# A grouped 1x1 convolution on one core: the small piece that only some DMA engines carry becomes larger and is shared with GpSimd's queue

## The chip, the core and the metric

The kernel runs on one core of a Trainium2 chip. The metric is the device time of one execution in microseconds (us), lower is better; the kernel before takes 485.12 us, the median of three runs that lie between 485.1 and 485.2. A core has TensorE for matmuls (PE in the profile), VectorE (DVE), ScalarE (ACT), GpSimd (POOL) and SyncE (SP), and its transfers between main memory and the on-chip memory are carried out by 16 DMA engines. An engine that issues a transfer puts it on a queue of its own; the 16 DMA engines work the queues off.

## The reference, cut to what matters

```python
H = W = 512; G = 4; Cg = 48; C = 192; k = 1
xg = x.reshape(B, H, W, G, Cg)                 # B = 1, bf16
out[..., g, :] = einsum('bhwc,cd->bhwd', xg[..., g, :], w[0, 0, :, g, :])
```

Each of 262,144 pixels has 192 channels in four groups of 48, and each group is multiplied by its own 48 x 48 matrix. A pixel is 384 bytes, so 100.66 MB are read and as many are written; the weights are small.

## The kernel before, in words

**Pieces.** All pixels are cut into pieces (`plan_pieces`, L67 to L86). A piece of n columns is a block of 128 rows (SBUF partitions) by n pixels; a column is thus one pixel in each of 128 rows. The middle of the image goes in pieces of 104 columns (`BIG`), ahead of them stand small head pieces of 8, 20 and 32 columns that share the first slot, so that work can begin early. One piece is different: the narrow one (`NARROW`, L32 to L34) has 48 columns but only 32 rows, 0 to 15 and 32 to 47, and each of its two 16-row blocks is handed over with a leading dimension of four (`a=4`, L114), so that four DMA engines carry it, 8 rows each. It stands in slot 10. With it the full pieces have 60 + 19 x 104 = 2036 columns instead of 2048; the 16 DMA engines carry those 2036 columns in equal shares, 8 rows each, and four of them another 48 columns' worth.

**The ring.** SBUF holds a ring of five slots of 104 columns (`ring`, L129). A slot is loaded, computed in place (the result is written over the input) and stored from.

**Queues.** SP issues all loads in order (L170 to L175); ahead of the load of slot n it waits until all stores of slot n - 5 have landed (L173). ACT issues all stores (`store`, L250 to L254) between its copies. Most pieces are stored with one transfer, the five slots before the last with two halves of 52, and the last slot in parts of 32, 32, 24 and 16 (L117 to L124). GpSimd only prepares two constants at the start (L155 to L162) and issues no transfer.

**Compute.** A group is 4 columns. For each group PE transposes six 128 x 128 blocks (L203), DVE copies the transposed blocks of a pair of groups to SBUF (L242), PE multiplies them by the weights (L218), and ACT copies the result over the input in the ring (L260). There are 521 groups. The first group of a piece waits for the load of the piece (L198). The narrow piece's 12 groups are computed with all 128 rows, though only 32 hold data.

Of the kernel before, what the change touches and what calls it, by code (L numbers as in the profile page):

```python
# [6 lines left out]
BF16 = mybir.dt.bfloat16  # L7
# [4 lines left out]
C = GROUPS * CG  # L12
# [11 lines left out]

BIG = 104
RCOLS = 5 * BIG
HEAD = (8, 20, 32)
LATE = 6
LATE_PARTS = (52, 52)
LAST_PARTS = (32, 32, 24, 16)  # L30
FULL = ((0, 128),)
NARROW = ((0, 16), (32, 16))  # L32
NARROW_COLS = 48
NARROW_AT = (9,)  # L34
NXP = 4
NXS = 3
NOB = 4
# [2 lines left out]
class Waiter:  # L40

    def __init__(self, eng):
        self.eng = eng
        self.seen = {}
# [5 lines left out]
        self.eng.wait_ge(sem, val)  # L50


class Piece:

    def __init__(self, i, slot, at, g0, size, blocks, pix):
        self.i, self.slot, self.at, self.size = i, slot, at, size
        self.g0, self.g1 = g0, g0 + size // 4
        self.full = blocks is FULL
        self.blocks = []
        for (r0, rows) in blocks:  # L60
            self.blocks.append((r0, rows, pix))
            pix += rows * size
        self.pix_end = pix
        assert size % 4 == 0 and self.at + size <= RCOLS


def plan_pieces(npix):  # L67
    few = NARROW_COLS * sum(rows for _, rows in NARROW)
    at = [i for i in NARROW_AT if npix >= len(NARROW_AT) * few + 128 * (sum(HEAD) + BIG * (i + 2))]
    cols = (npix - few * len(at)) // 128  # L70
    assert cols % 4 == 0
    head = list(HEAD) if cols >= sum(HEAD) + BIG else []
    mid = cols - sum(head)
    slots = [[(BIG, FULL)]] * (mid // BIG) + ([[(mid % BIG, FULL)]] if mid % BIG else [])
    for i in at:
        slots.insert(i, [(NARROW_COLS, NARROW)])
    if head:
        slots.insert(0, [(s, FULL) for s in head])
    pieces, g, pix = [], 0, 0
    for n, parts in enumerate(slots):  # L80
        c = n * BIG % RCOLS
        for s, blocks in parts:
            pieces.append(Piece(len(pieces), n, c, g, s, blocks, pix))
            c, g, pix = c + s, pieces[-1].g1, pieces[-1].pix_end
    assert pix == npix
    return pieces  # L86


def bass_standalone__grouped__vision_kernel(nc, x, w, out):
    B, H, W_, Cx = x.shape  # L90
    assert Cx == C and tuple(w.shape) == (1, 1, GROUPS, CG, CG)
    npix = B * H * W_
    assert npix % 512 == 0, "the pixel count must be a multiple of 512"

    pieces = plan_pieces(npix)
# [4 lines left out]
    xf = x.rearrange("b h w c -> (b h w) c")  # L100
    of = out.rearrange("b h w c -> (b h w) c")
# [2 lines left out]
    def groups(pair):  # L104
        return range(2 * pair, min(2 * pair + 2, NG))

    def transfers(ap, ring, p, c0=0, c1=None):
        c1 = c1 or p.size
        for (r0, rows, pix) in p.blocks:
            px = ap[pix:pix + rows * p.size, :]  # L110
            if p.full:
                view = px.rearrange("(p i) n -> p (i n)", p=rows)[:, c0 * C:c1 * C]
            else:
                view = px.rearrange("(c a i) n -> a c (i n)", a=4, c=rows // 4)  # L114
            yield view, ring[r0:r0 + rows, (p.at + c0) * C:(p.at + c1) * C]

    stores = []  # L117
    for p in pieces:
        late = pieces[-1].slot - p.slot
        parts = LAST_PARTS if late == 0 else LATE_PARTS if late < LATE else (BIG,)  # L120
        c = 0
        for n in parts if p.size == BIG and p.full else (p.size,):
            stores.append((p, c, c + n, p.g0 + (c + n) // 4))
            c += n  # L124
    st_val = {p: 16 * sum(len(p.blocks) for q, *_ in stores if q is p) for p in pieces}

    with ExitStack() as es:
        block = es.enter_context(nc.Block())
# [9 lines left out]
        def sem(name):  # L138
            return es.enter_context(nc.semaphore(name))

        ld_sem = [sem(f"ld{p.i}") for p in pieces]
        st_sem = [sem(f"st{p.i}") for p in pieces]
        w_sem, id_sem, e_sem, wb_sem, wc_sem = (sem(s) for s in ("w_sem", "id_sem", "e_sem", "wb_sem", "wc_sem"))
        p0_sem, p1_sem = sem("p0_sem"), sem("p1_sem")
        t_done, mm_done = sem("t_done"), sem("mm_done")
        e_done, fa_done = sem("e_done"), sem("fa_done")

        def columns(g):
            p = piece_of[g]
            at = p.at + 4 * (g - p.g0)  # L150
            return ring[:, at * C:(at + 4) * C]

        @block.gpsimd
        def _(gp):
            gp.memset(esel[:], 1.0).then_inc(p0_sem, 1)  # L155
            gp.memset(ident[:], 1.0).then_inc(p1_sem, 1)  # L156
            gp.wait_ge(p0_sem, 1)
            gp.affine_select(out=esel[:], in_=esel[:], pattern=[[-1, ECOLS]],  # L158
                             compare_op=AluOpType.is_equal, fill=0.0, base=ESHIFT,
                             channel_multiplier=1).then_inc(e_sem, 1)  # L160
            gp.wait_ge(p1_sem, 1)
            gp.affine_select(out=ident[:], in_=ident[:], pattern=[[-1, 128]],  # L162
                             compare_op=AluOpType.is_equal, fill=0.0, base=0,
                             channel_multiplier=1).then_inc(id_sem, 1)

        @block.sync
        def _(sp):
            wq = Waiter(sp)
            sp.dma_start(w_sb[:], wv).then_inc(w_sem, 16)  # L169
            for p in pieces:  # L170
                for q in pieces:
                    if q.slot == p.slot - RCOLS // BIG:
                        wq.wait(st_sem[q.i], st_val[q])  # L173
                for dram, sbuf in transfers(xf, ring, p):
                    sp.dma_start(sbuf, dram).then_inc(ld_sem[p.i], 16)  # L175

        @block.tensor
        def _(pe):
            wq = Waiter(pe)

            def build_weights():
                wq.wait(e_sem, 1)
                wq.wait(w_sem, 16)
                last = None
                for (tc, r, g, c0_) in WBLOCKS:
                    s0 = ESHIFT - r
                    col = WOFF[tc] + c0_
                    last = pe.matmul(o_ps[:, NOB - 1, col:col + CG], lhsT=esel[:, s0:s0 + 128],  # L188
                                     rhs=w_sb[:, g, :], start=True, stop=True, skip_group_check=True)
                last.then_inc(wb_sem, 1)  # L190

            def transposes(pair):
                wq.wait(e_done, pair - 1)
                last = None
                for g in groups(pair):
                    p = piece_of[g]
                    if g == p.g0:
                        wq.wait(ld_sem[p.i], 16 * len(p.blocks))  # L198
                    xg = columns(g)
                    for ul in range(2):  # L200
                        for tc in range(3):
                            j = ul * 3 + tc
                            last = pe.transpose(xT_ps[:, g % NXP, j * 128:(j + 1) * 128],  # L203
                                                xg[:, j * 128:(j + 1) * 128], ident[:])
                last.then_inc(t_done, 1)

            def matmuls(pair):
                wq.wait(e_done, pair + 1)
                for g in groups(pair):
                    xs = xT_sb[pair % NXS][:, g % 2 * 2 * UC:(g % 2 + 1) * 2 * UC]  # L210
                    wq.wait(fa_done, g - 1)
                    last = None
                    for ul in range(2):
                        v = 2 * g + ul
                        for tc in range(3):
                            j = ul * 3 + tc
                            c0_, c1_ = COLR[tc]
                            last = pe.matmul(o_ps[:, v % NOB, c0_:c1_], lhsT=xs[:, j * 128:(j + 1) * 128],  # L218
                                             rhs=wt[:, WOFF[tc]:WOFF[tc] + (c1_ - c0_)],
                                             start=(tc == 0), stop=(tc == 2), skip_group_check=True)  # L220
                    last.then_inc(mm_done, 1)

            build_weights()
            wq.wait(id_sem, 1)
            transposes(0)
            wq.wait(wc_sem, 1)
            for pair in range(NP):
                if pair + 1 < NP:
                    transposes(pair + 1)
                matmuls(pair)  # L230
# [14 lines left out]
        @block.scalar  # L245
        def _(act):
            wq = Waiter(act)
            todo = list(stores)

            def store():  # L250
                p, c0, c1, g1 = todo.pop(0)
                wq.wait(fa_done, g1)
                for dram, sbuf in transfers(of, ring, p, c0, c1):
                    act.dma_start(dram, sbuf).then_inc(st_sem[p.i], 16)  # L254

            for g in range(NG):
                wq.wait(mm_done, g + 1)
                v = 2 * g
                dst = columns(g).rearrange("p (u c) -> p u c", u=2)
                act.copy(dst, o_ps[:, v % NOB:v % NOB + 2, 0:UC]).then_inc(fa_done, 1)  # L260
                while todo and todo[0][3] <= g:
                    store()
            while todo:
                store()
            for p in pieces:
                wq.wait(st_sem[p.i], st_val[p])
# [28 lines left out]
```

## Time and profile before

| | us |
|---|---|
| median of three runs | 485.12 |
| span of the profiled execution, first to last instruction | 483.3 |
| PE busy | 431.3 |
| ACT busy | 392.6 |
| DVE busy | 250.2 |
| POOL busy | 1.3 |

The profiled execution has no other time of its own than its span; the median lies 1.8 us above it, which is what surrounds the first and the last instruction. The profile's page gives the busy time of each engine, the span in 40 slices with the mean busy share of the 16 DMA engines in each, the DMA queues, the chain of work that ended last, and the groups of instructions. Of the DMA engines the profile shows the mean share only, not each engine by itself; at the end of the span, where nothing new is issued, a share of n sixteenths means that n of the engines still run. Stretches of the span can be asked for by their start and end.

### The profile page before, as it was taken

To read this page: it belongs to the slowest core of one execution; us is meant where nothing else is said; L and a number is where in the kernel's file an instruction comes from. 1 tells how busy PE (TensorE), PEld (TensorE's weight loads), DVE (VectorE), ACT (ScalarE), POOL (GpSimd) and SP (SyncE) were. 2 spreads that over 40 slices of the span, in tenths; PEclk is the share of its full clock that TensorE was granted. 3 is DMA by queue.
4 is the path that set the end of the run, shared out by engine and by line. 5 is a ranking of instruction groups with operands and counts; after the bars stand their busy time and mean duration, and the time that the engine had idled before them with its cause. 6 is when DMAs were issued, how large, how long until landed. Compare 5 with 4: busy or idle time off the path is not lost.

```text
span 483.3 us, 13933 instructions
## 1 busy us (share of the span) xinstructions
PE 431.3 (89%) x6262; PEld 392.1 (81%) x6262; DVE 250.2 (52%) x262; ACT 392.6 (81%) x522; POOL 1.3 (0%) x8
## 2 busy tenths in 40 slices
PE   5699999999999999998599999979998999999910
PEld 5599888898898889887588988969787898899800
DVE  2345655656555565564256555544554655556500
ACT  2669999999999999998299999877888999999920
POOL 1000000000000000000000000000000000000000
PEclk9979999999999999999799999998999999999965
DMA  8999999999999999999999999999999999999993
GB/s 351 431 406 421 449 425 421 422 424 442 434 428 419 425 420 439 425 434 424 431 434 437 424 431 428 432 431 426 434 428 428 430 424 422 439 416 427 429 390 156
DMA packets 7834, 202.23 MB, mean 418 GB/s; under 512 B 1056, under 2 KB 1056, under 8 KB 1696
## 3 DMA queue, kind: packets, MB, share of 16 engines
q10 hardware_dynamic: 4360, 100.67, 48.7%
q1 hardware_dynamic: 3416, 100.68, 48.7%
q8 instruction: 50, 0.82, 0.6%
q14 instruction: 8, 0.07, 0.0%
HBM read 100.68 MB, written 100.66 MB: 417 GB/s over the span
## 4 chain that ended last, share of the span: by engine, by line
PE 54%; DMA 39%; ACT 1%; issue 1%; SPq 0%; ACTq 0%
PE o_ps L218 31%; PE xT_ps L203 22%; DMA ring<-in_x_dram 20%; DMA out_dram<-ring 19%; ACT ring L260 1%; SPq L175 0%; ACTq L254 0%; SPq L169 0%
## 5 line engine op out<-in xcount | busy, mean ns | idle before, releaser
L260 ACT CAST ring<-o_ps 128x768 bf16<-128x768 f32 x521 | 391.3, 802 | 68.5 <-PE o_ps L218 61.0
L242 DVE COPY xT_sb<-xT_ps 128x1536 bf16<-128x1536 bf16 (+1 forms) x261 | 249.6, 956 | 206.0 <-PE xT_ps L203 206.0
L218 PE MATMUL o_ps<-wt,xT_sb 128*128 128x144 bf16 (+1 forms) x3126 | 292.0, 236 | 5.9 <-ACT ring L260 1.3
L218 PEld LDWEIGHTS o_ps<-wt,xT_sb 128*128 128x128 bf16 x3126 | 212.0, 99 | 43.4 <-ACT ring L260 30.2
L203 PE MATMUL xT_ps<-ident,ring 128*128 128x128 bf16 x3126 | 222.7, 221 | 21.1 <-DMA ring<-in_x_dram 21.1
L203 PEld LDWEIGHTS xT_ps<-ident,ring 128*128 128x128 bf16 x3126 | 191.1, 99 | 22.7 <-DMA ring<-in_x_dram 19.8
L188 PE MATMUL o_ps<-w_sb,esel 48*128 48x48 bf16 x10 | 0.6, 210 | 2.7 <-DMA w_sb<-in_w_dram 2.7
L188 PEld LDWEIGHTS o_ps<-w_sb,esel 48*128 48x128 bf16 x10 | 0.5, 113 | 2.6 <-POOL esel L158 2.6
L236 DVE CAST wt<-o_ps 128x480 bf16<-128x480 f32 x1 | 0.7, 658 | 3.3 <-PE o_ps L188 3.3
L260 ACT ACT_TABLE_LOAD x1 | 1.3, 1283 | 0.8 <-PEq L280 0.8
L158 POOL TENSOR_SCALAR_AFFINE_SELECT esel<-esel 48x272 bf16<-48x272 bf16 x1 | 0.4, 405 | 0.0
L155 POOL MEMSET esel<- 48x272 bf16 x1 | 0.3, 318 | 0.3 <-POOLq L280 0.3
L162 POOL TENSOR_SCALAR_AFFINE_SELECT ident<-ident 128x128 bf16<-128x128 bf16 x1 | 0.3, 285 | 0.0
L156 POOL MEMSET ident<- 128x128 bf16 x1 | 0.2, 198 | 0.0
L280 POOL MEMSET const-bfloat16-1.0<- 128x1 bf16 x1 | 0.1, 102 | 0.0
L280 POOL MEMSET const-uint8-127<- 128x1 uint8 x1 | 0.1, 102 | 0.0
L280 POOL MEMSET const-float32-0.0<- 128x1 f32 x1 | 0.1, 98 | 0.3 <-issue 0.3
L280 POOL MEMSET const-float32-1.0<- 128x1 f32 x1 | 0.1, 98 | 0.0
## 6 DMA issues: line engine op xcount, KB each, us to landing
ring<-in_x_dram SPq DMA_DIRECT2D x19, 4992.0 KB, 37.5
out_dram<-ring ACTq DMA_DIRECT2D x13, 4992.0 KB, 45.5
out_dram<-ring ACTq DMA_DIRECT2D x10, 2496.0 KB, 47.7
out_dram<-ring ACTq DMA_DIRECT2D x3, 1536.0 KB, 19.7
ring<-in_x_dram SPq DMA_DIRECT2D x1, 1536.0 KB, 8.4
out_dram<-ring ACTq DMA_DIRECT2D x1, 1152.0 KB, 16.6
ring<-in_x_dram SPq DMA_DIRECT2D x1, 960.0 KB, 5.2
out_dram<-ring ACTq DMA_DIRECT2D x1, 960.0 KB, 28.6
```

The lines of the kernel that those rows point to most:

```text
L155: gp.memset(esel[:], 1.0).then_inc(p0_sem, 1)
L156: gp.memset(ident[:], 1.0).then_inc(p1_sem, 1)
L158: gp.affine_select(out=esel[:], in_=esel[:], pattern=[[-1, ECOLS]], compare_op=AluOpType.is_equal, fill=0.0, base=ESHIFT, channel_multipli ...
L162: gp.affine_select(out=ident[:], in_=ident[:], pattern=[[-1, 128]], compare_op=AluOpType.is_equal, fill=0.0, base=0, channel_multiplier=1) ...
L188: last = pe.matmul(o_ps[:, NOB - 1, col:col + CG], lhsT=esel[:, s0:s0 + 128], rhs=w_sb[:, g, :], start=True, stop=True, skip_group_check=True)
L203: last = pe.transpose(xT_ps[:, g % NXP, j * 128:(j + 1) * 128], xg[:, j * 128:(j + 1) * 128], ident[:])
L218: last = pe.matmul(o_ps[:, v % NOB, c0_:c1_], lhsT=xs[:, j * 128:(j + 1) * 128], rhs=wt[:, WOFF[tc]:WOFF[tc] + (c1_ - c0_)], start=(tc == ...
L236: dve.tensor_copy(wt[:], o_ps[:, NOB - 1, 0:WCOLS]).then_inc(wc_sem, 1)
L242: dve.tensor_copy(xT_sb[pair % NXS][:, 0:n * 2 * UC].rearrange("p (g c) -> p g c", g=n), xT_ps[:, b0:b0 + n, 0:2 * UC]).then_inc(e_done, 1)
L260: act.copy(dst, o_ps[:, v % NOB:v % NOB + 2, 0:UC]).then_inc(fa_done, 1)
L280: nc = _bacc.Bacc("TRN2", target_bir_lowering=False, num_devices=1)
```

## The change

The narrow piece is replaced by a shared one in the same slot 10. It has two kinds of blocks, which differ in columns and in the queue that carries them:

- rows 0 to 15 and 32 to 47 by 72 columns (before: 48), issued by SP and stored by ACT as before, on DMA engines 0 to 3 by the words of the change;
- rows 52 to 95 (44 rows) by 64 columns, loaded and stored by GpSimd's queue, with a leading dimension of 11, on DMA engines 5 to 15 by the words of the change. Ahead of each of the two GpSimd transfers stands a small transfer of 5 rows (2 x 64 bytes each) into a buffer that nobody reads (`cur`); it is there to set the engine with which the next transfer begins.

GpSimd waits for the free slot as SP does, issues the load, waits until ACT has copied the last group of the piece, and issues the store. PE waits for both loads ahead of the piece's first group. SP, ahead of the load of slot 15, waits for both stores of slot 10.

The numbers that follow from the plan: the shared piece holds 32 x 72 + 44 x 64 = 5120 pixels instead of 1536, so the full pieces have 2008 columns instead of 2036. The heads are 8, 20, 28 and 32 columns, then come 18 full pieces of 104 and a last one of 48 columns in slot 20 (before: 104). Since the last piece isn't of 104 columns, it is stored with one transfer of 48 columns. There are 520 groups instead of 521, of which the shared piece has 18 (narrow: 12).

```diff
-HEAD = (8, 20, 32)
+HEAD = (8, 20, 28, 32)
-FULL = ((0, 128),)
-NARROW = ((0, 16), (32, 16))
-NARROW_COLS = 48
-NARROW_AT = (9,)
+SHARED_AT = (9,)
+SHARED_COLS = 72
+SYNC, POOL = 0, 1
+SHARED = ((0, 16, 4, SHARED_COLS, SYNC), (32, 16, 4, SHARED_COLS, SYNC), (52, 44, 11, 64, POOL))
+CURSOR = 5
...
+                view = px.rearrange("(c a i) n -> a c (i n)", a=b.parts, c=b.rows // b.parts)
+            yield view, ring[b.r0:b.r0 + b.rows, (p.at + e0) * C:(p.at + e1) * C]
...
+        def wait_slot(wq, p):
+            for q in pieces:
+                if q.slot == p.slot - RCOLS // BIG:
+                    wq.wait(st_sem[q.i], st_val[q])
+                    if q in pl_sem:
+                        wq.wait(ps_sem[q], pool_val[q])
...
+            def pool_dmas(p, ap, inward, done):
+                for dram, sbuf in transfers(ap, ring, p, POOL):
+                    n = turns[0]
+                    few = xf[0:CURSOR, 0:128].rearrange("p (a b) -> p a b", a=2)[:, :, 0:32]
+                    gp.dma_start(cur[:, n], few).then_inc(cur_sem, 16)
+                    turns[0] += 1
+                    gp.dma_start(*((sbuf, dram) if inward else (dram, sbuf))).then_inc(done, 16)
+
+            for p in pooled:
+                wait_slot(wq, p)
+                pool_dmas(p, xf, True, pl_sem[p])
+                wq.wait(fa_done, p.g1)
+                pool_dmas(p, of, False, ps_sem[p])
...
-                        wq.wait(ld_sem[p.i], 16 * len(p.blocks))
+                        wq.wait(ld_sem[p.i], 16 * len(p.on(SYNC)))
+                        if p in pl_sem:
+                            wq.wait(pl_sem[p], pool_val[p])
```

More of the change, by code (lines that the diff above doesn't have):

```diff
@@ L50, in wait, with __init__, on @@
         self.eng.wait_ge(sem, val)
+class Block:
+    def __init__(self, r0, rows, parts, cols, queue, pix):
+        self.r0, self.rows, self.parts, self.cols, self.queue, self.pix = r0, rows, parts, cols, queue, pix
 class Piece:
-    def __init__(self, i, slot, at, g0, size, blocks, pix):
+    def __init__(self, i, slot, at, g0, size, shares, pix):
         self.i, self.slot, self.at, self.size = i, slot, at, size
         self.g0, self.g1 = g0, g0 + size // 4
-        self.full = blocks is FULL
+        self.full = shares is None
         self.blocks = []
-        for (r0, rows) in blocks:
-            self.blocks.append((r0, rows, pix))
-            pix += rows * size
+        for (r0, rows, parts, cols, queue) in shares or ((0, 128, 1, size, SYNC),):
+            self.blocks.append(Block(r0, rows, parts, cols, queue, pix))
+            pix += rows * cols
         self.pix_end = pix
         assert size % 4 == 0 and self.at + size <= RCOLS
+    def on(self, queue):
+        return [b for b in self.blocks if b.queue == queue]
 def plan_pieces(npix):
-    few = NARROW_COLS * sum(rows for _, rows in NARROW)
-    at = [i for i in NARROW_AT if npix >= len(NARROW_AT) * few + 128 * (sum(HEAD) + BIG * (i + 2))]
+    few = sum(rows * cols for _, rows, _, cols, _ in SHARED)
+    at = list(SHARED_AT)
+    if npix < len(at) * few + 128 * (sum(HEAD) + BIG * (at[-1] + 2)):
+        at = []
     cols = (npix - few * len(at)) // 128
@@ L73, in plan_pieces @@
     mid = cols - sum(head)
-    slots = [[(BIG, FULL)]] * (mid // BIG) + ([[(mid % BIG, FULL)]] if mid % BIG else [])
+    slots = [[(BIG, None)]] * (mid // BIG) + ([[(mid % BIG, None)]] if mid % BIG else [])
     for i in at:
-        slots.insert(i, [(NARROW_COLS, NARROW)])
+        slots.insert(i, [(SHARED_COLS, SHARED)])
     if head:
-        slots.insert(0, [(s, FULL) for s in head])
+        slots.insert(0, [(s, None) for s in head])
     pieces, g, pix = [], 0, 0
@@ L81, in plan_pieces @@
         c = n * BIG % RCOLS
-        for s, blocks in parts:
-            pieces.append(Piece(len(pieces), n, c, g, s, blocks, pix))
+        for s, shares in parts:
+            pieces.append(Piece(len(pieces), n, c, g, s, shares, pix))
             c, g, pix = c + s, pieces[-1].g1, pieces[-1].pix_end
@@ L105, in groups, with transfers @@
         return range(2 * pair, min(2 * pair + 2, NG))
[L107 to L112, printed above, removed]
-            else:
-                view = px.rearrange("(c a i) n -> a c (i n)", a=4, c=rows // 4)
-            yield view, ring[r0:r0 + rows, (p.at + c0) * C:(p.at + c1) * C]
+    def transfers(ap, ring, p, queue, c0=0, c1=None):
+        for b in p.on(queue):
+            px = ap[b.pix:b.pix + b.rows * b.cols, :]
+            e0, e1 = c0, min(c1 or b.cols, b.cols)
+            if b.parts == 1:
+                view = px.rearrange("(p i) n -> p (i n)", p=b.rows)[:, e0 * C:e1 * C]
+            else:
+                view = px.rearrange("(c a i) n -> a c (i n)", a=b.parts, c=b.rows // b.parts)
+            yield view, ring[b.r0:b.r0 + b.rows, (p.at + e0) * C:(p.at + e1) * C]
     stores = []
@@ L124, in bass_standalone__grouped__vision_kernel @@
             c += n
-    st_val = {p: 16 * sum(len(p.blocks) for q, *_ in stores if q is p) for p in pieces}
+    st_val = {p: 16 * sum(len(p.on(SYNC)) for q, *_ in stores if q is p) for p in pieces}
+    pooled = [p for p in pieces if p.on(POOL)]
+    pool_val = {p: 16 * len(p.on(POOL)) for p in pooled}
     with ExitStack() as es:
@@ L142, in bass_standalone__grouped__vision_kernel @@
         st_sem = [sem(f"st{p.i}") for p in pieces]
+        pl_sem = {p: sem(f"pl{p.i}") for p in pooled}
+        ps_sem = {p: sem(f"ps{p.i}") for p in pooled}
+        cur_sem = sem("cur_sem")
+        cur = es.enter_context(nc.sbuf_tensor("cur", [CURSOR, 2 * len(pooled), 2, 32], BF16))
         w_sem, id_sem, e_sem, wb_sem, wc_sem = (sem(s) for s in ("w_sem", "id_sem", "e_sem", "wb_sem", "wc_sem"))
@@ L151, in columns @@
             return ring[:, at * C:(at + 4) * C]
+        def wait_slot(wq, p):
[4 more added lines that the diff above has]
+                        wq.wait(ps_sem[q], pool_val[q])
         @block.gpsimd
         def _(gp):
+            wq = Waiter(gp)
             gp.memset(esel[:], 1.0).then_inc(p0_sem, 1)
@@ L164, in _ @@
                              channel_multiplier=1).then_inc(id_sem, 1)
+            turns = [0]
+            def pool_dmas(p, ap, inward, done):
[10 more added lines that the diff above has]
+                pool_dmas(p, of, False, ps_sem[p])
+            for p in pooled:
+                wq.wait(ps_sem[p], pool_val[p])
+            wq.wait(cur_sem, 16 * turns[0])
         @block.sync
@@ L170, in _ @@
             for p in pieces:
[L171 to L174, printed above, removed]
+                wait_slot(wq, p)
+                for dram, sbuf in transfers(xf, ring, p, SYNC):
                     sp.dma_start(sbuf, dram).then_inc(ld_sem[p.i], 16)
@@ L252, in store @@
                 wq.wait(fa_done, g1)
-                for dram, sbuf in transfers(of, ring, p, c0, c1):
+                for dram, sbuf in transfers(of, ring, p, SYNC, c0, c1):
                     act.dma_start(dram, sbuf).then_inc(st_sem[p.i], 16)
```

## The prediction

> **What bounds the kernel now.** I read the page's slices and queues first: is anything idle, and who carries the bytes?
>
> ```profile
> span 483.3 us, 13933 instructions
> DMA  8999999999999999999999999999999999999993
> ...
> q10 hardware_dynamic: 4360, 100.67, 48.7%
> q1 hardware_dynamic: 3416, 100.68, 48.7%
> q8 instruction: 50, 0.82, 0.6%
> ```
>
> The DMA engines are the busy resource in every slice, from the first to the last but one. Loads (q1) and stores (q10) take 97.4% of the time of 16 engines. The next view is the windows: one over the middle, then the end cut finely.
>
> ```profile
> core 0: us, PE busy (x) PEld busy (x) DVE busy (x) ACT busy (x) POOL busy (x), PEclk, DMA share, GB/s
> 30.00:180.00 150.00, 148.35 (x2206) 134.98 (x2204) 88.03 (x92) 137.54 (x184) 0.00 (x0) 1.00 1.01 428
> 240.00:460.00 220.00, 209.60 (x3072) 190.00 (x3072) 122.68 (x129) 192.63 (x257) 0.00 (x0) 0.99 1.00 429
> 463.00:466.00 3.00, 0.00 (x0) 0.00 (x0) 0.00 (x0) 0.00 (x0) 0.00 (x0) 0.50 1.03 439
> 467.00:474.00 7.00, 0.00 (x0) 0.00 (x0) 0.00 (x0) 0.00 (x0) 0.00 (x0) 0.50 0.80 341
> 476.70:477.20 0.50, 0.00 (x0) 0.00 (x0) 0.00 (x0) 0.00 (x0) 0.00 (x0) 0.50 0.30 129
> 477.60:479.20 1.60, 0.00 (x0) 0.00 (x0) 0.00 (x0) 0.00 (x0) 0.00 (x0) 0.50 0.19 79
> 479.50:480.40 0.90, 0.00 (x0) 0.00 (x0) 0.00 (x0) 0.00 (x0) 0.00 (x0) 0.50 0.11 48
> 480.60:482.20 1.60, 0.00 (x0) 0.00 (x0) 0.00 (x0) 0.00 (x0) 0.00 (x0) 0.50 0.06 27
> 482.40:483.30 0.90, 0.00 (x0) 0.00 (x0) 0.00 (x0) 0.00 (x0) 0.00 (x0) 0.50 0.00 0
> ```
>
> The last two columns carry the argument. In the middle the share is 1.0: no engine waits for work. At the end times 16 it counts the engines that still run: 16 until 466, then 13 (0.80), 5 (0.30), 3 (0.19), 2 (0.11), 1 (0.06), none. Three engines are done at about 466.5, one runs alone from 480.5 to 482.3, at 27 GB/s. Since engines are never idle, each one's end is the sum of its own work. Compute is over by then:
>
> ```profile
> 459.52 2.35 ACT L260 CAST ring<-o_ps 128x768 bf16<-128x768 f32 x3
> 461.90 0.34 ACTq L254 DMA_DIRECT2D out_dram<-ring  x1
> ...
> out_dram<-ring ACTq DMA_DIRECT2D x1, 768.0 KB, 20.9
> ```
>
> The last store is issued at 461.9 and lands 20.9 us later, though its 16 columns are under 2 us of work: it queues. So the slowest DMA engine sets the time, not PE or ACT.
>
> **The price of a column.** One engine moves 27 GB/s (the row of the last one). A column is 8 rows of 384 bytes per engine, 3072 bytes: 0.114 us one way, 0.228 us in and out. Check: 2036 columns are 464 us, from a start at about 2 us to 466.5, the end of the three that finish first. They carry nothing else.
>
> **Who ends last.** Engines 0 to 3 carry 48 columns more, 48 x 0.228 = 10.9 us; none of them can end before 466.5 + 10.9 = 477.4. Five engines are still running at 477, so these are the four and one odd engine that has only 2036 columns and yet is over 10 us behind its equals. I take the odd one to be the last, at 482.3, and the last of the four the one before it, at 480.5. Following single packets in the trace back to back (no view prints them), the chain that ends last holds none of the narrow piece's rows. The other order is a rival.
>
> **The change, engine by engine** (full columns and shared ones; 44 rows on 11 engines are 4 rows each, so 64 columns count as 32):
>
> - Engines 0 to 3: 2036 + 48 = 2084 becomes 2008 + 72 = 2080. Four columns less, -0.9 us: the last of them at 479.6.
> - Engine 4: 2036 becomes 2008, 28 less, -6.4 us. If it is the odd one, it ends at 475.9.
> - Engines 5 to 15: 2036 becomes 2008 + 32 = 2040, +0.9 us. All of them but the odd one were done by 476.7, so by 477.6.
>
> The new end is that of engines 0 to 3, 479.6 instead of 482.3: **-2.7 us**. What was next late before is the bound now.
>
> **Unknown prices.** The trace before has no GpSimd transfer; I bound them.
>
> ```profile
> ring<-in_x_dram SPq DMA_DIRECT2D x1, 384.0 KB, 3.3
> out_dram<-ring ACTq DMA_DIRECT2D x1, 384.0 KB, 17.1
> w_sb<-in_w_dram SPq DMA_DIRECT2D x1, 18.0 KB, 1.7
> ```
>
> - A GpSimd row of 24.6 KB on an engine: not cheaper than 27 GB/s, since the bytes move on the same engines. From above, the dearest packets of the page: q8 moves 0.82 MB in 0.6% of 16 x 483.3 us = 46 us, 17.7 GB/s, 1.53 times the price. That adds 0.53 x 32 x 0.228 = 3.9 us to engines 5 to 15 (481.5). I take the lower price: rows of 24.6 KB are nearer to the load and store rows than to the instruction packets.
> - The two small transfers on engines 0 to 4: from nothing to 1.7 us each, the whole landing of the weights. A 384 KB load has 0.9 us of work per engine and lands after 3.3 us, so 2.4 us of a landing are no engine time; the weights' 1.7 are nearly all of that kind. I take 0.1 us for both.
>
> **Edits at no cost, and their cover.** PE's work is one group less, at 150 / 184 = 0.815 us per group of the window above. The wait for the shared load stands here:
>
> ```profile
> 182.25 64.80 SPq L175 DMA_DIRECT2D ring<-in_x_dram  x5
> ...
> 227.26 0.50 PE L203 MATMUL xT_ps<-ident,ring 128*128 128x128 bf16 x6
> 234.57 0.82 PE L203 MATMUL xT_ps<-ident,ring 128*128 128x128 bf16 x6 [6.81 <-DMA ring<-in_x_dram]
> ...
> SPq L175 <- DMA out_dram<-ring: 342.7, 15, 31.6
> ```
>
> SP gets slot 10 at 182.25. PE ends its 12 groups at 227.3, so it began them at 217.5, 35 us after the issue; in the new kernel seven more head groups stand ahead. GpSimd waits for the same stores and has nothing ahead in its queue; its rows are 3.6 us of work per engine, 11 if it gets one turn in three. That is covered by 24 us. Behind PE's new wait stand its own transposes and the matmuls of the pair before; behind GpSimd's waits stands nothing. SP's wait for GpSimd's store holds the load of slot 15 and those behind it, but the narrow store, queued behind full ones on ACT's queue, must land there anyway; SP waits 342.7 us in all without an idle DMA engine, since four other slots are in flight.
>
> The last store grows from 16 to 48 columns, 5.5 us of work instead of 1.8. The three first engines ended 4.6 us after its issue, 2.8 beyond its work; now they end 8.3 after it. Only if compute ended after 479.6 - 8.3 = 471.3, 9.4 us later than now, would this decide. The extra head piece only reorders loads that keep the engines busy from the start.
>
> **Sum.** -2.7 + 0.1 = -2.6 us on the span of 483.3; the 1.8 us between span and median stay: 485.12 - 2.6 = **482.5**.
>
> **Two rules of the Trainium skill.** "DMA: Bandwidth & Descriptors", section "Why a DMA increments its semaphore by 16 and not by 1", says that a transfer uses the largest number of engines up to 16 that divides the outer dimension of both sides, on GpSimd's queue consecutive ones from a round-robin position; that supports 5 engines and then 11. It also says that this queue was seen to give some copies 16 engines with rows / 16 rounded up; that is the third rival here. The same page, section "Latency and other measured facts", names engines 7 and 15 as usually behind the others; that is the first rival. No row here names an engine.
>
> **The rivals.**
>
> 1. The odd engine is not engine 4 but one of 5 to 15. It gains 4 columns: 482.3 + 0.9 = 483.2, time 486.0. For it: no row tells its number. By the packets it has no instruction packets (q8) either, nor have the three that finish first, while eight engines do; were those eight 8 to 15, it would be one of 4 to 7. That it is 4 is my choice.
> 2. One of engines 0 to 3 ends last and the odd one earlier: 482.3 - 0.9, time 484.2. Against it: the packets.
> 3. GpSimd's rows fall elsewhere, **slower**. If 44 rows go out as three each over fifteen engines, engines 0 to 3 get 3 x 64 / 8 = 24 columns more, 2104 in all, 20 above now: 480.5 + 4.6 = 485.1, time 487.9. If the position doesn't start at 0, a group of 11 covers some of engines 0 to 3: 2112 columns, +6.4, 486.9, time 489.7. It makes the kernel slower from 1.8 us on, 8 columns above today's 2084. No row speaks for or against.
> 4. GpSimd's rows at the upper price: 481.5, time 484.3.
> 5. Compute gets late past 471.3, through a wait for the shared load or for slot 15: each us beyond is one us. Against it: 9.4 us in hand.
>
> **Chances.** Forecast 0.62; rivals 2 and 4 together 0.08; rival 1 0.11; rival 3 0.14 (0.05 by the spread over fifteen engines, 0.09 by the position); rival 5 and others 0.05. A measurement of this kernel tells about 0.2% from no change, 0.97 us. Faster: 0.62, half of rivals 2 and 4, some of the rest, 0.68. Same: the other half and half of rival 1, 0.10. Slower: the rest, 0.22. Range: the last of engines 0 to 3 ends 3 us behind the earliest end possible for it; if 1 us of that falls elsewhere, 481.3 is the low end; the high end takes in rivals 4, 2 and 1, 486.1. It leaves out rival 3 and part of 5.
>
> **What would show it.** Right: the span ends near 480.7; the count of running engines still goes down by three first (at 467 to 470), no engine runs alone as long as 1.8 us, and the last four end between 476 and 480. GpSimd's load lands within 15 us of its issue and PE doesn't wait ahead of slot 10. Wrong: one engine alone to 483 (rival 1), several to 485 or 487 (rival 3), a share below 1.0 in the middle (rival 5).

## The result, and the profile after

The changed kernel takes 483.10 us (median of four runs, 482.60 to 483.69), the one before 485.11 us beside it (485.08 to 485.20): a ratio of 0.9957 with a 95% interval of 0.9943 to 0.9971, so 0.43% faster, 0.29 to 0.57%. The forecast was 482.5 us. The spans of the four executions are 480.4, 480.8, 481.0 and 481.1 us, against 480.7 forecast.

The page of the changed kernel, the lines that answer to those shown of before:

```profile
span 480.8 us, 13914 instructions
...
DMA  8999999999999999999999999999999999999995
...
q1 hardware_dynamic: 3560, 99.60, 48.5%
q10 hardware_dynamic: 4072, 99.58, 48.5%
q0 software_dynamic: 224, 2.16, 1.1%
q8 instruction: 49, 0.80, 0.6%
```

q0 is GpSimd's queue: 1.08 MB in and as much out, taken from q1 and q10. Its packets took 1.1% of 16 x 480.8 us, 85 us for 2.16 MB, 25.5 GB/s per engine (24.4 to 26.7 by the rounding of the 1.1%). That is near the price of ordinary rows (27), not that of the instruction packets (17.7). The last slice has risen from 3 to 5 tenths: the engines end closer together. The same windows at the end of the span; the last two columns are the share of the 16 DMA engines and GB/s:

```profile
core 0: us, PE busy (x) PEld busy (x) DVE busy (x) ACT busy (x) POOL busy (x), PEclk, DMA share, GB/s
240.00:460.00 220.00, 204.31 (x2964) 185.46 (x2964) 117.79 (x123) 185.69 (x248) 1.10 (x2) 0.98 1.00 429
463.00:466.00 3.00, 0.00 (x0) 0.00 (x0) 0.00 (x0) 0.00 (x0) 0.00 (x0) 0.50 1.02 438
470.00:474.00 4.00, 0.00 (x0) 0.00 (x0) 0.00 (x0) 0.00 (x0) 0.00 (x0) 0.50 0.84 359
476.00:477.00 1.00, 0.00 (x0) 0.00 (x0) 0.00 (x0) 0.00 (x0) 0.00 (x0) 0.50 0.30 129
478.00:479.00 1.00, 0.00 (x0) 0.00 (x0) 0.00 (x0) 0.00 (x0) 0.00 (x0) 0.50 0.09 37
479.00:480.00 1.00, 0.00 (x0) 0.00 (x0) 0.00 (x0) 0.00 (x0) 0.00 (x0) 0.50 0.09 37
480.00:480.80 0.80, 0.00 (x0) 0.00 (x0) 0.00 (x0) 0.00 (x0) 0.00 (x0) 0.50 0.00 0
```

There is still no idle engine in the middle (1.00). Three engines again stop first, now at about 469 (0.84 is 13 engines). From 478 on only one to two run (37 GB/s), and nobody runs alone to 482. Following single packets, which no view prints, the last two are engines of the four that carry the 72-column rows, both done at 480.0; the engine with the lag carries neither those rows nor GpSimd's and ends at 476.2. Forecast were 479.6 and 475.9. The windows bear out the 480.0; which engine ends when rests on the packets alone.

GpSimd's transfers, in its timeline and in the list of issues (KB, median us from issue to landing):

```profile
190.75 0.70 POOL L197 DMA_DIRECT2D cur<-in_x_dram  x1 [188.79 <-DMA out_dram<-ring]
191.45 0.56 POOL L199 DMA_DIRECT2D ring<-in_x_dram  x1
245.89 0.55 POOL L197 DMA_DIRECT2D cur<-in_x_dram  x1 [53.88 <-ACT ring L304]
246.43 0.56 POOL L199 DMA_DIRECT2D out_dram<-ring  x1
...
ring<-in_x_dram POOLq DMA_DIRECT2D x1, 1056.0 KB, 19.3
out_dram<-ring POOLq DMA_DIRECT2D x1, 1056.0 KB, 25.7
...
cur<-in_x_dram POOLq DMA_DIRECT2D x2, 0.6 KB, 9.4
```

The load lands 19.3 us after its issue, at 210.8, later than the 15 us that I named, but some 10 us before PE comes to the shared piece (18 groups of 0.815 us ahead of the wait that begins at 236.0). PE's only wait in this part is, as before, the one for the full piece in slot 11, 5.72 instead of 6.81 us. ACT issues the last store at 460.67 instead of 461.90:

```profile
241.70 1.46 PE L247 MATMUL xT_ps<-ident,ring 128*128 128x128 bf16 x12 [5.72 <-DMA ring<-in_x_dram]
...
460.67 0.34 ACTq L298 DMA_DIRECT2D out_dram<-ring  x1
```

### The profile page after: what moved, and what is told of

The parts are those of the page before. It is cut to its first block, busy times and chain, and to the rows that moved or that the text cites. A ratio compares the mean times of both kernels' runs of the same rounds, so it can differ in the third digit from the quotient of the medians.

```text
span 480.8 us, 13914 instructions
## 1 busy us (share of the span) xinstructions
PE 430.3 (89%) x6250; PEld 390.5 (81%) x6250; DVE 249.6 (52%) x261; ACT 391.9 (81%) x521; POOL 3.7 (1%) x12
## 3 DMA queue, kind: packets, MB, share of 16 engines
q0 software_dynamic: 224, 2.16, 1.1%
## 4 chain that ended last, share of the span: by engine, by line
PE 47%; another core or an unknown queue 24%; DMA 23%; SPq 1%; issue 1%; ACT 0%
PE o_ps L262 27%; PE xT_ps L247 20%; DMA ring<-in_x_dram 13%; DMA out_dram<-ring 10%; SPq L217 1%; ACT ring L304 0%; SPq L213 0%; SPq L51 0%
## 5 line engine op out<-in xcount | busy, mean ns | idle before, releaser
L286 DVE COPY xT_sb<-xT_ps 128x1536 bf16<-128x1536 bf16 x260 | 249.0, 958 | 205.1 <-PE xT_ps L247 205.1
L262 PEld LDWEIGHTS o_ps<-wt,xT_sb 128*128 128x128 bf16 x3120 | 210.8, 98 | 43.1 <-ACT ring L304 32.8
L197 POOL DMA_DIRECT2D cur<-in_x_dram x2 | 1.2, 622 | 242.7 <-DMA out_dram<-ring 188.8
```

The source lines that it names most:

```text
L197: gp.dma_start(cur[:, n], few).then_inc(cur_sem, 16)
L286: dve.tensor_copy(xT_sb[pair % NXS][:, 0:n * 2 * UC].rearrange("p (g c) -> p g c", g=n), xT_ps[:, b0:b0 + n, 0:2 * UC]).then_inc(e_done, 1)
```

## The experiments

**The theory** is that of the prediction: the time is the end of the DMA engine with the most work, at 0.228 us per column, and engine 4 has some 16 us of lag of its own, which the change relieves. The rivals: another engine has the lag, or the gain comes from somewhere else (the smaller last piece, the ring, compute).

**1. Put engine 4 back in, leave engine 15 out.**

```diff
-SHARED = (..., (52, 44, 11, 64, POOL))
+SHARED = (..., (48, 44, 11, 64, POOL))
-                    few = xf[0:CURSOR, 0:128]...
+                    rows = CURSOR - 1 if inward else CURSOR
+                    few = xf[0:rows, 0:128]...
```

> The 44-row block moves from rows 52 to 95 to rows 48 to 91, and the small transfers are of 4 rows ahead of the load and 5 ahead of the store, so that engines 4 to 14 carry it and engine 15 is left out. Theory (the time is the end of the DMA engine with the most work, and engine 4 is the one with about 16 us of lag of its own): engine 4 goes from 2008 to 2040 columns, 32 x 0.228 = 7.3 us more, from 476 to 483.3; time 486.0 to 486.5, slower than the kernel before. Rival (another engine than 4 is the odd one, or none is, and the gain came from something else in the plan): no engine passes 480.3, time stays at 483.1.

Measured: 486.26 us, ratio to before 1.0022 (1.0013 to 1.0032). The end of the span:

```profile
span 484.1 us, 13914 instructions
...
477.00:479.00 2.00, 0.00 (x0) 0.00 (x0) 0.00 (x0) 0.00 (x0) 0.00 (x0) 0.50 0.24 101
480.30:482.20 1.90, 0.00 (x0) 0.00 (x0) 0.00 (x0) 0.00 (x0) 0.00 (x0) 0.50 0.11 49
482.40:482.90 0.50, 0.00 (x0) 0.00 (x0) 0.00 (x0) 0.00 (x0) 0.00 (x0) 0.50 0.09 37
```

Four engines run at 478, two at 481, and work goes on past 482.4. The same number of bytes, the same queue, the same plan, one engine further down: 3.2 us more than the changed kernel. The rival that the gain comes from the plan as such falls. The sum has one engine alone past 480.3, though, and here two run past 481; where the second comes from is open. The next experiment isolates one engine.

**2. Show the lag without GpSimd.** Two versions of the kernel before, with a narrow piece of 64 columns on four and on five engines:

```diff
-LAST_PARTS = (32, 32, 24, 16)
+LAST_PARTS = (32, 32, 16, 16)        # four engines: (32, 32, 20, 16)
-NARROW = ((0, 16), (32, 16))
-NARROW_COLS = 48
+NARROW = ((0, 20), (32, 20))         # five engines; four keep (0, 16), (32, 16)
+NARROW_COLS = 64
...
-                view = px.rearrange("(c a i) n -> a c (i n)", a=4, c=rows // 4)
+                view = px.rearrange("(c a i) n -> a c (i n)", a=5, c=rows // 5)    # five engines only
...
-        for n in parts if p.size == BIG and p.full else (p.size,):
+        for n in parts if p.size >= 96 and p.full else (p.size,):
```

Four engines:

> The kernel before without any GpSimd transfer, its narrow piece 64 columns wide instead of 48 (four engines); full pieces 2032 columns, the last piece of 100 columns stored in parts of 32, 32, 20 and 16. Theory: engines 0 to 3 carry 2096 instead of 2084 columns, 480.5 + 2.7 = 483.2, engine 4 only 4 columns less, 481.4; time 486.0. So without the GpSimd share the larger blocks lose. Rival (a smaller full part is what helps): below 485.1.

Five engines:

> The same with five engines: rows 0 to 19 and 32 to 51 by 64 columns, leading dimension 5; full pieces 2028 columns, last piece of 96 columns stored in parts of 32, 32, 16 and 16. Theory (engine 4 is the one with about 16 us of lag of its own): engine 4 goes from 2036 to 2092 columns, 482.3 + 56 x 0.228 = 495.1, time 497.9. Rival (the odd engine is another): engines 0 to 4 carry 2092 columns, the last at 482.3, the odd one 1.8 us earlier than before; time 485.1.

Measured: 485.89 us with four (1.0018, 1.0009 to 1.0028) and 497.69 us with five (1.0260, 1.0243 to 1.0277). The five-engine kernel at its end:

```profile
span 495.8 us, 13986 instructions
...
481.00:483.00 2.00, 0.00 (x0) 0.00 (x0) 0.00 (x0) 0.00 (x0) 0.00 (x0) 0.50 0.11 48
485.00:494.00 9.00, 0.00 (x0) 0.00 (x0) 0.00 (x0) 0.00 (x0) 0.00 (x0) 0.50 0.06 26
```

One engine runs alone (0.06, 26 GB/s) for over 9 us. Adding the fifth engine to a piece cost 11.8 us, though each of the other four carries 4 columns less. From the kernel before (485.16 beside it), the fifth engine's 56 columns cost 497.69 - 485.16 = 12.5 us, 0.224 us each. So the lag is that of the fifth engine that these queues use, engine 4 by the change's numbering, and GpSimd has no part in it. The four-engine kernel shows that larger blocks alone lose.

**3. Move the load of engines 0 to 3 up and down.**

```diff
-SHARED_COLS = 72
+SHARED_COLS = 88        # and 56 in the other; GpSimd's block stays 44 x 64
...
-        slots.insert(i, [(SHARED_COLS, SHARED)])
+        slots.insert(i, [(64, SHARED)])      # with 56 only
```

The last two lines give the piece with 56 columns the 64 that GpSimd's block needs, so it has 16 groups; with 88 columns it has 22, in the changed kernel 18.

88 columns:

> The blocks on engines 0 to 3 get 88 columns instead of 72; the full pieces have 2004 columns. Theory (engines 0 to 3 end last in the changed kernel): they carry 2092 instead of 2080, 12 x 0.228 = 2.7 us more; span 483.5, time 485.8, all the gain gone, while engines 5 to 15 end 0.9 us earlier. Rival (GpSimd's queue, compute or the one large last store sets the end): no more than 483.1, since those have less to do or the same.

56 columns:

> The blocks on engines 0 to 3 get 56 columns instead of 72; the full pieces have 2012 columns. Theory: engines 0 to 3 carry 2068 instead of 2080, 2.7 us less, ending at 477.6; engines 5 to 15 carry 4 columns more, the last of them at 478 to 478.6, and engine 4 is at 477.1. The engines with the instruction packets become the bound: span 479.0 to 479.4, time 481.3 to 481.8. Rival (GpSimd's queue, compute or the one large last store sets the end): 483.1 or 0.9 us more.

Measured: 485.86 us with 88 (1.0017, 1.0007 to 1.0026) and **481.93 us with 56** (0.9937, 0.9920 to 0.9954). The first meets the theory's 485.8, the second lies 0.1 us above its range of 481.3 to 481.8. Engines 0 to 3 are the bound of the changed kernel; with 56 columns, by the sum, the next group is. The end with 56 columns:

```profile
476.00:477.00 1.00, 0.00 (x0) 0.00 (x0) 0.00 (x0) 0.00 (x0) 0.00 (x0) 0.50 0.60 260
477.00:478.00 1.00, 0.00 (x0) 0.00 (x0) 0.00 (x0) 0.00 (x0) 0.00 (x0) 0.50 0.14 60
478.00:479.00 1.00, 0.00 (x0) 0.00 (x0) 0.00 (x0) 0.00 (x0) 0.00 (x0) 0.50 0.05 20
```

About ten engines run at 476.5 (0.60) and nearly all of them stop within 1 us, where the changed kernel has five. One engine runs on past 478 (0.05); which one, no view tells. This version beats the kernel before. By its median it is also 1.2 us under the changed one; the two ratios' intervals overlap, but the spans of the four executions of each don't (479.0 to 479.9 against 480.4 to 481.1).

**4. Leave the small transfers out.**

```diff
-                    gp.dma_start(cur[:, n], few).then_inc(cur_sem, 16)
-                    turns[0] += 1
```

> The changed kernel without the two small transfers ahead of GpSimd's load and store. Theory (GpSimd's queue goes round the engines from a position that starts at engine 0): the load falls on engines 0 to 10, the store on 11 to 15 and 0 to 5, so engines 0 to 3 carry 2008 + 72 + 32 = 2112 columns, 7.3 us more than now; span 487.5, time 490.4. Rival 1 (the position doesn't matter, the rows are spread some other way): 483.1, or up to 2 us more. Rival 2 (the position outlives an execution, 22 engines further each time): executions of the same kernel differ by several us, between 483 and 490.

Measured: 491.51 us (1.0129, 1.0114 to 1.0144), single executions from 490.86 to 491.71. Near the theory's 490.4 and steady, so the position does not wander over these four executions, and the small transfers are what the gain hangs on. At the end several engines are late together:

```profile
484.00:486.00 2.00, 0.00 (x0) 0.00 (x0) 0.00 (x0) 0.00 (x0) 0.00 (x0) 0.50 0.21 92
486.00:487.00 1.00, 0.00 (x0) 0.00 (x0) 0.00 (x0) 0.00 (x0) 0.00 (x0) 0.50 0.09 37
```

At 485 three to four engines run, as if engines 0 to 3 carry the surplus. The 1.1 us beyond the sum are not explained; spans of 488.3 to 489.6 us show that they lie inside the span.

**5. What else could have mattered.** Three kernels: the last 48 columns stored in three parts; GpSimd's block in rows 84 to 127; the kernel before with two small GpSimd transfers that nobody needs.

```diff
-        for n in parts if p.size == BIG and p.full else (p.size,):
+        for n in parts if p.size == BIG and p.full else (16,) * 3 if late == 0 else (p.size,):
```

> The changed kernel with the last piece's 48 columns stored in three transfers of 16 instead of one. Theory (engines 0 to 3 are busy without a gap until they end): 483.1, within 0.4 us. Rival (the one large last store, issued only when all is computed, sets the end): 3.6 us less at most, 479.5 to 482.5.

```diff
-SHARED = (..., (52, 44, 11, 64, POOL))
+SHARED = (..., (84, 44, 11, 64, POOL))
```

> The changed kernel with the 44-row block in rows 84 to 127 instead of 52 to 95; the engines that carry it stay 5 to 15, but they are no longer those that carry the same rows of the full pieces. Theory: the work of each engine is the same and engines 0 to 3 don't touch these rows: 483.1, within 0.4 us. Rival (rows and engines have to match, or the engines hinder each other): GpSimd's rows take up to 1.5 times as long, engines 5 to 15 end up to 3.9 us later, time up to 484.5, and the packets of that queue take longer than in the changed kernel.

```diff
+            for n, g in enumerate((narrow.g0 - 30, narrow.g1)):
+                gp.wait_ge(fa_done, g)
+                gp.dma_start(cur[:, n], few).then_inc(cur_sem, 16)
+            gp.wait_ge(cur_sem, 32)
```

> The kernel before, with its narrow piece unchanged, plus two of the small GpSimd transfers (5 rows of 2 x 64 bytes), one 30 groups ahead of the narrow piece and one after it; nobody needs their data. Theory: no work for the engines to speak of; span as before, 483.3. What lies around the span was 1.8 us before and is 2.1 to 2.3 us in every kernel with GpSimd transfers; if using GpSimd's queue at all costs that, the time is 485.4 to 485.6. Rival (the extra 0.4 us come from the plan with four heads and one last store): 485.1. Rival 2 (small transfers hold up engines 0 to 4): over 486.

Measured: 483.53 us with the split store (0.9964, 0.9951 to 0.9976), 483.68 with the other rows (0.9966, 0.9954 to 0.9979), 485.31 with the small transfers (1.0001, 0.9992 to 1.0009). The intervals of all three ratios overlap with those of their parent kernels, though the split store lies just above the 0.4 us that the theory allowed and the other rows 0.2 us above it. The last store doesn't set the end. Where the rows lie matters by less than these runs can tell: GpSimd's packets take 1.1% of the engines' time with either place. Two small GpSimd transfers by themselves cost nothing: the theory's 485.4 to 485.6 for them was wrong.

**6. A better cut, which failed.**

```diff
-SHARED = ((0, 16, 4, SHARED_COLS, SYNC), (32, 16, 4, SHARED_COLS, SYNC), (52, 44, 11, 64, POOL))
+SHARED = ((0, 16, 4, 58, SYNC), (32, 16, 4, 58, SYNC),
+          (20, 12, 3, 64, POOL), (64, 32, 8, 54, POOL), (52, 12, 3, 64, POOL))
```

> The same shares idea, cut by what each group of engines has left in the profile of the changed kernel: engines 0 to 3 carry 58 columns (SP and ACT), engines 5 to 7 rows 20 to 31 and 52 to 63 by 64 columns, engines 8 to 15 rows 64 to 95 by 54 columns (GpSimd, with small transfers of 5, 5 and 8 rows per direction to place them); full pieces stay at 2008 columns. Theory, with engines 5 to 7 taken to be the three that finish first: engines 0 to 3 go from 2080 to 2066 columns, end 480.0 - 3.2 = 476.8; engine 4 stays at 476.2; engines 5 to 7 from 2040 to 2072, 475.8 to 476.5; engines 8 to 15 from 2040 to 2035, 476.6. Span 477.4 to 477.8, time 479.7 to 480.2. Rival 1 (the three that finish first are others than 5 to 7): one of the other engines gets 7.3 us more than it can bear, span over 483, time over 485. Rival 2 (each GpSimd transfer costs the engines something of its own; there are twelve instead of four): 480.5 to 482.

Measured: 487.33 us (1.0041, 1.0029 to 1.0053), single executions from 485.94 to 488.35. Rival 1's figures are met (span over 483, time over 485). GpSimd issues the five-row transfer and its third block at 192.68 and 193.24; PE gets the piece at 240.7:

```profile
192.68 0.56 POOL L198 DMA_DIRECT2D cur<-in_x_dram  x1
193.24 0.56 POOL L206 DMA_DIRECT2D ring<-in_x_dram  x1
...
240.71 1.44 PE L257 MATMUL xT_ps<-ident,ring 128*128 128x128 bf16 x12 [18.28 <-DMA ring<-in_x_dram]
...
474.53 0.34 ACTq L308 DMA_DIRECT2D out_dram<-ring  x1
...
ring<-in_x_dram POOLq DMA_DIRECT2D x2, 288.0 KB, 32.4
cur<-in_x_dram POOLq DMA_DIRECT2D x2, 1.0 KB, 57.0
...
470.00:474.00 4.00, 3.16 (x41) 2.36 (x38) 1.35 (x2) 3.85 (x6) 0.00 (x0) 1.00 0.67 285
474.00:476.00 2.00, 0.00 (x0) 0.00 (x0) 0.00 (x0) 0.50 (x1) 0.00 (x0) 1.00 0.51 220
480.00:481.00 1.00, 0.00 (x0) 0.00 (x0) 0.00 (x0) 0.00 (x0) 0.00 (x0) 0.50 0.78 332
481.00:482.00 1.00, 0.00 (x0) 0.00 (x0) 0.00 (x0) 0.00 (x0) 0.00 (x0) 0.50 0.13 55
482.00:483.00 1.00, 0.00 (x0) 0.00 (x0) 0.00 (x0) 0.00 (x0) 0.00 (x0) 0.50 0.09 37
```

PE waits 18.28 us, the third block lands 47 us after its issue, and the last store goes out at 474.5, 13.9 us later than in the changed kernel and past the 471.3 that the prediction named as the point. The share falls to 0.67 and 0.51 between 470 and 476: engines stand idle until the last store is issued, and most of them then end together at 481. So late compute sets the end of most engines. It does not set the end of the span in this execution: two engines go on to 482.9 and 483.2, and their packets follow one another without a gap of more than 0.01 us from 420 on. As far as packets can be followed, these are two of the three engines 5 to 7, which carry instruction packets, while one of the three does finish early. Rival 2 is not shown: what the many GpSimd transfers cost is time to land. The profiled execution is the fastest of the six (span 484.1); the others have spans of 485.0 to 486.5, and what lengthens them no trace shows. The failure tells nothing against the sum of work, but both assumptions that I built on it, which engines finish first and that compute stays clear, were wrong.

## Why the prediction was right, point by point

- **What bounds the kernel.** Right. Six kernels moved columns between engines (experiments 1 to 4); five came out within some 0.2 us of the time or the range worked out at 0.228 us per column, and the one without small transfers 1.1 us above it.
- **Engine 4 is the odd one.** I had chosen this, no row told it, so that it came true is luck; had it been one of 5 to 15, the time would have been rival 1's 486.0. Shown by experiments 1 and 2, which fit no other engine of 0 to 4 or 5 to 15. Rival 1 falls, and with it the use made of the Trainium skill, "DMA: Bandwidth & Descriptors", section "Latency and other measured facts", which has engines 7 and 15 as usually slower: the engine that lags here is neither of them. Rival 2 falls too: what ends last before is engine 4.
- **Engines 0 to 3 are the next bound.** Right: 479.6 forecast, 480.0 in the profiled execution, and experiment 3 moves the time with their load.
- **Where GpSimd's rows fall.** Eleven engines after five, from engine 0 in each execution: experiment 4 is off by 8.4 us without the small transfers. That agrees with the Trainium skill, "DMA: Bandwidth & Descriptors", section "Why a DMA increments its semaphore by 16 and not by 1", which has consecutive engines from a round-robin position; its other statement, of 16 engines for some copies, is not what these 44 rows got (rival 3's 487.9 against 483.10 measured). That the position starts at engine 0 each time fits the four executions of experiment 4.
- **The price of GpSimd's rows.** The lower bound was nearly right (25.5 GB/s; rival 4 falls). The wait for them was underrated: 11 us of turns, or 15 with reserve, against 19.3 measured. One turn in three among rows of unequal length is longer: four rows of 24.6 KB, each beside two of 40 KB, are some 15 us at 27 GB/s, an estimate. The cover held, so compute kept its reserve (rival 5), but experiment 6 shows how it is used up.
- **What was off.** The term "the 1.8 us between span and median stay". In the changed kernel they are 1.9 to 2.9 us, median 2.2, beside a median of 1.8 before (up to 2.4 in single executions); that is two thirds of the 0.6 us by which the forecast was low, the span is the rest (median 480.9 for 480.7). What lengthens it is open: two small GpSimd transfers don't (1.8, experiment 5), the kernel with 88 columns has 1.7 to 2.0 and the one without small transfers 2.0 to 3.0.

## What to carry to other kernels

Where all DMA engines are busy to the end, the mean share hides the bound: cut the last few per cent of the span into short windows, read the share as a count of engines, and add up what the share lacks to 1 from the first engine's end on; that is the most that moving rows between engines can give. Before the change it is between 7 and 8 us, an estimate from short windows of its trace between 466 and 482.3; the change took 2.0 of them, the version with 56 columns 3.2. How long the last engine runs alone, 1.8 us, only tells when the next one becomes the bound. Then price a move by the bytes of the one engine that ends last, and look at once at who is next, because the gain ends there. Before a share goes to chosen engines, show by one kernel that the numbering is as assumed: a wrong set of engines cost more here than the right one gave.

## What the runs showed of the hardware that I had not expected

One DMA engine of 16, engine 4, needs about 16 us more for the same 2036 columns than the three that carry nothing else (482.3 against 466.5 before the change), with GpSimd's queue and without (experiments 1 and 2, which ran on different chips). The packets of the kept traces, which no view prints, show where the time goes: into its stores. In the kernel with five engines, the engine that ends alone can be followed back; between 452 and 468 its stored rows of 19,968 bytes take 0.79 to 0.83 us each, most others 0.742, and from 472 on it takes 0.742 to 0.748 too. Before the change 165 of 2944 stored rows of 39,936 or 19,968 bytes are slow like this (1.53 to 1.66 and 0.75 to 0.90 us; one engine's part is 184), and what they take beyond the usual 1.476 and 0.742 us adds up to 14.7 us. That all of these are engine 4's was not followed, and why its stores are slow is open.

A GpSimd transfer of 0.6 KB takes 9.4 us to land beside busy SP and ACT queues, against 1.7 us for the 18 KB of weights on idle engines, and transfers issued behind one another on GpSimd's queue add up: in experiment 6 the third block took 47 us for 288 KB, and the 1.0 KB behind the blocks 57.0 us. Taking its place between two queues of 40 KB rows, one packet at a time, would explain that; it was not tried by itself.
